# MLP biases as a broadcast tensor operand instead of a per-partition scalar in the PSUM evacuations

## The chip, the cores and the metric

One core of one Trainium2 chip. The metric is device time in microseconds (us), from the first to the last instruction of the program on that core. Times of different kernels are compared only where they were taken in the same rounds on the same chip.

## The reference, cut to what matters

A transformer-like block: layer norm, 32-head attention and an MLP on the same normalised input, joined by a gate.

```python
def _A_ref(x, wqkv, wo):            # attention, S=2048, D=1024, 32 heads of 32
    ...
    p = _softmax(scores, axis=-1)
    o = jnp.einsum("bhqk,bhkd->bhqd", p, v)
    return ... @ wo

def _B_ref(x, w1, b1, w2, b2):      # MLP, F=3584
    y = _layernorm(x, axis=-1)
    h = _gelu(jnp.einsum("bsd,df->bsf", y, w1) + b1)
    return jnp.einsum("bsf,fd->bsd", h, w2) + b2

x = A_x
xn = _layernorm(x, axis=-1)
s = _A_ref(xn, A_wqkv, A_wo)
g = _silu(_B_ref(xn, B_w1, B_b1, B_w2, B_b2))
return x + s * g
```

The biases `b1` and `b2` belong to the feature, and the products are stored with features on the partitions. So within one tile a bias is one number per partition, the same for every column.

## The kernel before

Python builds a list of operations for each engine. A helper `op` records what an operation reads and writes, sets the semaphore waits from that, and advances a small model clock by the cost `c` (in ns). The model clock decides where deferred VectorE work (square, cube, gate) and the tanh of ScalarE are put between the rest.

The main loop runs 512 units. In each, TensorE computes attention scores (`s_unit`, line 869 of the kernel), then one piece of a projection or MLP product (line 395), then the attention-value products of the unit before (lines 898 and 901). ScalarE takes the exponentials (line 881). All pieces in the main part accumulate in one PSUM bank, number 7: before the next product may write there, VectorE must have read the last one out. (PSUM is where TensorE's products are written in this kernel, `ps` in the profile; reading a finished product out of it is called its evacuation here.)

```python
def fin(bk):                                   # first MLP product, one of 168 evacuations
    ...
    take(kx, ku)
    run_dq(pg.ready("vector", r=[("b", bk)]) + TOL)      # deferred VectorE work that fits
    x0 = op("vector", lambda e: e.tensor_scalar(xb[:, 0:n], bank(bk, 0, n), b1T[:, f:f + 1], None, op0=ALU.add),
       r=[("b", bk), "b1"], w=[kx], c=217 + 1.042 * n)   # line 548
    ...
    later(square, x0.t + 34.0, (m2, 0))        # deferred: square, cube; then tanh on ScalarE, then gate
```
```python
def fin(bk):                                   # second MLP product, one of 48 evacuations
    ...
    x0 = op("vector", lambda e: e.tensor_scalar(zh[:, 0:n], bank(bk, 0, n), 0.25, b2h[:, nb:nb + 1], op0=ALU.mult, op1=ALU.add),
       r=[("b", bk), "b2"], w=[kz], c=217 + 1.042 * n)   # line 605
```

The width `n` is 352 columns in two thirds of the pieces and 320 in one third.

The softmax here doesn't subtract the row's maximum and nothing guards it: scores larger than these inputs give would overflow.

## Time and profile before

| | before |
|---|---|
| time, median of 4 runs (1089.04 to 1090.72) | 1089.69 us |
| span of the profiled run | 1086.9 us |
| TensorE busy | 1077.7 us, 99% |
| ScalarE busy | 1043.6 us, 96% |
| VectorE busy | 627.6 us, 58% |
| chain that ended last | PE 57%, ACT 42% |

Three of those four runs were known when the prediction was written; their median was 1089.52. A busy share says how full an engine is; the chain says whose work the end waited for. VectorE is on neither list as a bound. In the profile's lines PE is TensorE, PEld its loads of weights (29156, as many as matmuls; one opens each product), DVE VectorE and ACT ScalarE; L548 is line 548 of the kernel.

### The profile page before, as it was taken

What the parts mean: (1) busy time and instruction counts of PE and PEld (TensorE: products, weight loads), DVE (VectorE), ACT (ScalarE), POOL (GpSimd) and SP (SyncE); (2) the same over time, 40 slices, a digit from 0 to 9 for tenths busy, and PEclk for the clock granted to TensorE, in tenths of its full rate; (3) what the DMA queues carried; (4) which work ended last, traced back from release to release, by engine and by line L of the source; (5) the groups of instructions that cost most, each with busy time, mean ns of one, the idle gap of its engine ahead of it and who ended that gap; (6) DMA issues with size and microseconds to landing.
All of it is one profiled execution on the core that took longest, in us unless ns stands there. A gap on an engine that the chain in (4) does not pass through costs nothing.

```text
span 1086.9 us, 61820 instructions
## 1 busy us (share of the span) xinstructions
PE 1077.7 (99%) x29156; PEld 701.4 (65%) x29156; DVE 627.6 (58%) x1396; ACT 1043.6 (96%) x1197; POOL 22.5 (2%) x69
## 2 busy tenths in 40 slices
PE   9999999999999999999999999999999999999998
PEld 6766666666666666666666666666666666666665
DVE  8488843477732576642377743378733387635556
ACT  7899998999999999999999999999999999999993
POOL 4400000000000000000000000000000000000000
PEclk9999999999999999999999999999999999999999
DMA  8944355413474224345233264423264243685444
GB/s 243 178 134 139 116 165 154 126 52 110 118 155 123 67 60 125 104 104 149 90 100 102 70 165 113 125 81 109 81 132 119 91 119 108 194 202 110 108 92 124
DMA packets 209336, 131.92 MB, mean 121 GB/s; under 512 B 52538, under 2 KB 200250, under 8 KB 209082
## 3 DMA queue, kind: packets, MB, share of 16 engines
q1 hardware_dynamic: 209082, 127.97, 43.5%
q8 instruction: 228, 3.74, 1.5%
q14 instruction: 26, 0.21, 0.1%
HBM read 104.87 MB, written 12.06 MB: 108 GB/s over the span
## 4 chain that ended last, share of the span: by engine, by line
PE 57%; ACT 42%; DVE 0%; DMA 0%; issue 0%; POOL 0%; SPq 0%
ACT P L881 38%; PE ps L395 33%; PE ps L869 9%; PE ps L898 6%; PE ps L901 6%; ACT u L565 3%; PE ps L687 1%; PE ps L703 1%; ACT thz L609 0%; DMA OT<-in_A_x_dram 0%; PE ps L386 0%; DVE wq L669 0%; ACT hT L714 0%; DVE zh L605 0%; DVE wq L671 0%
## 5 line engine op out<-in xcount | busy, mean ns | idle before, releaser
L881 ACT ACTIVATE P<-ps 128x1024 bf16<-128x1024 f32 x1024 | 968.1, 1080 | 8.7 <-PE ps L869 3.9
L898 PE MATMUL ps<-P,VP 128*32 128x256 bf16 x4096 | 256.4, 273 | 0.0
L901 PE MATMUL ps<-P,ones 128*32 128x256 bf16 x4096 | 256.3, 273 | 0.0
L395 PE MATMUL ps<-yTc,war 128*32 128x352 bf16 (+1 forms) x5376 | 225.5, 309 | 0.5 <-issue 0.5
L395 PE MATMUL ps<-hT,war 128*32 128x352 bf16 (+1 forms) x5376 | 225.3, 309 | 0.0
L869 PE MATMUL ps<-QT,KT 32*128 32x256 bf16 x4096 | 203.3, 273 | 2.7 <-ACT P L881 0.2
L395 PEld LDWEIGHTS ps<-yTc,war 128*32 128x32 bf16 x5376 | 127.4, 96 | 74.9 <-DVE xb L548 19.2
L395 PEld LDWEIGHTS ps<-hT,war 128*32 128x32 bf16 x5376 | 127.9, 96 | 73.9 <-issue 25.1
L869 PEld LDWEIGHTS ps<-QT,KT 32*128 32x128 bf16 x4096 | 60.7, 92 | 114.4 <-issue 60.4
L605 DVE TENSOR_SCALAR zh<-ps,b2h 128x352 f32<-128x352 f32 (+1 forms) x48 | 27.4, 572 | 182.6 <-PE ps L395 182.6
L548 DVE TENSOR_SCALAR xb<-ps,b1T 128x352 f32<-128x352 f32 (+1 forms) x168 | 96.2, 573 | 48.9 <-PE ps L395 43.9
L571 DVE SCALAR_TENSOR_TENSOR hT<-u,xb 128x352 bf16<-128x352 f32 (+1 forms) x168 | 84.4, 510 | 67.6 <-ACT u L565 67.6
L898 PEld LDWEIGHTS ps<-P,VP 128*32 128x32 bf16 x4096 | 109.3, 97 | 20.4 <-issue 1.3
L901 PEld LDWEIGHTS ps<-P,ones 128*32 128x32 bf16 x4096 | 109.2, 97 | 18.7
L395 PE MATMUL ps<-xnT,wq 128*32 128x352 bf16 (+1 forms) x2688 | 112.7, 309 | 0.0
L395 PEld LDWEIGHTS ps<-xnT,wq 128*32 128x32 bf16 x2688 | 63.7, 96 | 37.2 <-DVE xb L548 9.1
L558 DVE SCALAR_TENSOR_TENSOR u<-u,xb 128x352 f32<-128x352 f32 (+1 forms) x168 | 82.5, 509 | 1.9
L554 DVE TENSOR_TENSOR u<-xb 128x352 f32<-128x352 f32 (+1 forms) x168 | 82.5, 507 | 0.7
L565 ACT ACTIVATE u<-u 128x704 f32<-128x704 f32 (+1 forms) x84 | 71.4, 855 | 0.0
L395 PE MATMUL ps<-xnT,OT 128*32 128x352 bf16 (+2 forms) x1568 | 62.9, 306 | 0.2 <-DVE wq L669 0.2
L395 PE MATMUL ps<-wq,xnT 128*32 128x256 bf16 x1536 | 50.8, 274 | 0.0
L395 PEld LDWEIGHTS ps<-xnT,OT 128*32 128x32 bf16 x1568 | 37.7, 96 | 19.9 <-DVE wq L669 7.7
(61 smaller groups left out, 478.6 us busy)
## 6 DMA issues: line engine op xcount, KB each, us to landing
war<-in_B_w_dram SPq DMA_DIRECT2D x336, 256.0 KB, 3.3
wq<-in_A_wqkv_dram SPq DMA_DIRECT2D x36, 128.0 KB, 2.5
OT<-in_A_x_dram SPq DMA_DIRECT2D x16, 256.0 KB, 5.6
xnT<-in_A_x_dram SPq DMA_DIRECT2D x16, 256.0 KB, 3.2
out_dram<-wq SPq DMA_DIRECT2D x15, 256.0 KB, 2.0
y_scratch<-OT SPq DMA_DIRECT2D x14, 256.0 KB, 2.5
gT_scratch<-gst SPq DMA_DIRECT2D x32, 88.0 KB, 3.2
xnT<-in_A_wo_dram SPq DMA_DIRECT2D x8, 256.0 KB, 4.3
```

The costliest lines, as they stand in the source:

```text
L395: ins = e.matmul(outs(j), lhsT=lhs(j), rhs=rhs, start=start, stop=stop, tile_position=(0, 32 * j), skip_group_check=True)
L548: x0 = op("vector", lambda e: e.tensor_scalar(xb[:, 0:n], bank(bk, 0, n), b1T[:, f:f + 1], None, op0=ALU.add), r=[("b", bk), "b1"], w=[kx] ...
L554: x = op("vector", lambda e: e.tensor_tensor(ub[:, 0:n], xb[:, 0:n], xb[:, 0:n], op=ALU.mult), r=[kx], w=[ku], c=151 + 1.042 * n)
L558: x = op("vector", lambda e: e.scalar_tensor_tensor(ub[:, 0:n], ub[:, 0:n], 1.0 / 0.044715, xb[:, 0:n], op0=ALU.add, op1=ALU.mult), r=[kx, ...
L565: x = op("scalar", lambda e: e.activation(ut[:, :, 0:n], ut[:, :, 0:n], ACT.Tanh, scale=0.7978845608028654 * 0.044715), r=kus, w=kus, c=48 ...
L571: op("vector", lambda e: e.scalar_tensor_tensor(hT[:, fq, 0:n], ut[:, i, 0:n], 1.0, xq[:, 0:n], op0=ALU.add, op1=ALU.mult), r=[kus[i], kq] ...
L605: x0 = op("vector", lambda e: e.tensor_scalar(zh[:, 0:n], bank(bk, 0, n), 0.25, b2h[:, nb:nb + 1], op0=ALU.mult, op1=ALU.add), r=[("b", bk ...
L687: ins = e.matmul(bank(bk, off, off + 256), lhsT=wq[:, which, dc, 0:128], rhs=xnT[:, dc, t0:t0 + 256], start=dc == 0, stop=dc == DC - 1, sk ...
L869: ins = e.matmul(bank(bks[j], kh * 256, (kh + 1) * 256), lhsT=KT[i2][32 * j:32 * j + 32, k0:k0 + 128], rhs=QT[i2][32 * j:32 * j + 32, qb * ...
L881: op("scalar", lambda e, p=p, sl=sl: e.activation(pb[:, 2 * p:2 * p + 2, :, :].rearrange("p a b q -> p (a b q)"), ps[:, sl * 1024:(sl + 1) ...
L898: e.matmul(bankq(ACC, j, 0, QW), lhsT=VP[vp][:, kb, vo + 32 * j:vo + 32 * j + 32], rhs=pb[:, j, kh, :], start=first, stop=False, tile_posi ...
L901: ins = e.matmul(bankq(ACC, j, QW, 2 * QW), lhsT=ones[:, 0:32], rhs=pb[:, j, kh, :], start=False, stop=last, tile_position=(0, 32 * j), sk ...
```

## The change

The intent is to shorten the evacuations that add a bias. The per-partition scalar becomes an ordinary second tensor operand, whose access pattern repeats the one bias of each partition over all columns. The builder's cost of the two evacuations goes from 217 to 165 ns plus 1.042 ns per column.

```diff
-                x0 = op("vector", lambda e: e.tensor_scalar(xb[:, 0:n], bank(bk, 0, n), b1T[:, f:f + 1], None, op0=ALU.add),
-                   r=[("b", bk), "b1"], w=[kx], c=217 + 1.042 * n)
+                x0 = op("vector", lambda e: e.tensor_tensor(xb[:, 0:n], bank(bk, 0, n), b1T[:, f:f + 1].to_broadcast((128, n)), op=ALU.add),
+                   r=[("b", bk), "b1"], w=[kx], c=165 + 1.042 * n)
...
-                x0 = op("vector", lambda e: e.tensor_scalar(zh[:, 0:n], bank(bk, 0, n), 0.25, b2h[:, nb:nb + 1], op0=ALU.mult, op1=ALU.add),
-                   r=[("b", bk), "b2"], w=[kz], c=217 + 1.042 * n)
+                x0 = op("vector", lambda e: e.scalar_tensor_tensor(zh[:, 0:n], bank(bk, 0, n), 0.25, b2h[:, nb:nb + 1].to_broadcast((128, n)), op0=ALU.mult, op1=ALU.add),
+                   r=[("b", bk), "b2"], w=[kz], c=165 + 1.042 * n)
```

## The prediction

1089.52, the median known then, less 0.4 for the direct gain is 1089.1 us. The lengths of the new forms stand on the trace alone: 524 and 490 ns of line 669, and 526 and 492 as an estimate from lines 558 and 554 (519 and 518 ns). The 1 to 6 us allowed for the order, and so the range, follow from no measurement; what one misplaced tanh costs was not measured either. The "half rate" of rival 3 is a supposition; its 330 ns are an estimate, about what 320 columns take once more at the 1.03 ns of the trace.

> **What bounds the kernel now.** I read the page's busy shares first, then the chain of work that ended last, then the groups of VectorE by form, the waits, and last the timeline around single evacuations, because a busy share cannot tell whether a wait of 0.06 us is hidden.
>
> ```profile
> PE 1077.7 (99%) x29156; PEld 701.4 (65%) x29156; DVE 627.6 (58%) x1396; ACT 1043.6 (96%) x1197; POOL 22.5 (2%) x69
> ...
> PE 57%; ACT 42%; DVE 0%; DMA 0%; issue 0%; POOL 0%; SPq 0%
> ```
>
> TensorE and ScalarE are both nearly full and share the whole chain; VectorE, the only engine that the change touches, is 58% busy and has no share of the chain that rounds above 0%. The per-line figures of the chain agree: the bias evacuation of the first MLP product does not appear among the fifteen lines printed, and that of the second is there with 0%. The granted clock is 0.999, so no throttle hides anything.
>
> Next, what one bias evacuation costs beside its neighbours. The groups by form, with the mean in ns as the second number after the bar:
>
> ```profile
> L548 DVE TENSOR_SCALAR xb<-ps,b1T 128x352 f32<-128x352 f32 x112 | 65.4, 584 | 30.5 <-PE ps L395 26.6
> ...
> L548 DVE TENSOR_SCALAR xb<-ps,b1T 128x320 f32<-128x320 f32 x56 | 30.8, 551 | 18.3 <-PE ps L395 17.3
> ...
> L605 DVE TENSOR_SCALAR zh<-ps,b2h 128x352 f32<-128x352 f32 x32 | 18.7, 584 | 141.6 <-PE ps L395 141.6
> ...
> L669 DVE TENSOR_TENSOR wq<-ps,xnT 128x352 f32<-128x352 f32 x32 | 16.8, 524 | 19.4 <-PE ps L395 19.3
> ...
> L605 DVE TENSOR_SCALAR zh<-ps,b2h 128x320 f32<-128x320 f32 x16 | 8.8, 548 | 41.0 <-PE ps L395 41.0
> ```
>
> The two-tensor form from PSUM (L669, of the output projection) takes 524 ns on 352 columns; the form with a per-partition scalar takes 584. That difference of 60 ns is what the change is after.
>
> The waits show one reason to take it seriously. All projection and MLP products of the main part accumulate in the same PSUM bank, so the next product cannot start before the evacuation has read the bank:
>
> ```profile
> PEld ps L395 <- DVE xb L548: 34.7, 164, 0.3
> ...
> PEld ps L395 <- DVE zh L605: 10.1, 48, 0.2
> ```
>
> These are 44.8 us in 212 waits, 0.21 us each. They name VectorE, but 0.21 us is also what the weight loads idle when nothing is waited for ("issue": 29.6 us in 138 times, 0.21 each). So I looked at single instances. Two stretches of the timeline (start, length, engine, line):
>
> ```profile
> 411.35 0.42 DVE L435 CAST VP<-ps 128x256 bf16<-128x256 f32 x1
> ...
> 411.75 0.40 PE L869 MATMUL ps<-QT,KT 32*128 32x256 bf16 x8
> 412.07 0.94 PEld L395 LDWEIGHTS ps<-xnT,wq 128*32 128x32 bf16 x32 [0.21 <-issue]
> ```
> ```profile
> 702.78 0.58 DVE L548 TENSOR_SCALAR xb<-ps,b1T 128x352 f32<-128x352 f32 x1
> ...
> 703.10 0.40 PE L869 MATMUL ps<-QT,KT 32*128 32x256 bf16 x8
> ...
> 703.42 1.02 PEld L395 LDWEIGHTS ps<-yTc,war 128*32 128x32 bf16 x32 [0.21 <-DVE xb L548]
> ```
>
> In the first the evacuation is the short one and ends at 411.77, 0.30 us before the next product starts; in the second it is a biased one and ends at 703.36, 0.06 us before. Yet from the start of the score matmuls (L869) to the start of the next product it is 0.32 us in both. I collected that distance over the whole timeline for every product that follows score matmuls: the median is 0.33 us in each of the seven groups of evacuation (by line and width), and only 2 of the 216 biased evacuations are followed by a distance above 0.36 us (0.39 both times). The sum of all excess over 0.33 us, all groups together, is 0.23 us. So TensorE goes from score matmuls to the next product in its own 0.33 us, and the biased evacuation ends 0.06 us (352 columns) or 0.09 us (320) before that runs out. **It is hidden, by a narrow margin.**
>
> [...] L669 takes 524 and 490. [...] (584 - 551)/32 = 1.03 ns per column for the form of now. [...] Here one bank serves, and the overlap is with the attention matmuls in between; the trace shows it suffices. [...]
>
> **The change, part by part.**
> First MLP product (168 evacuations): a TENSOR_SCALAR with a pointer to the bias becomes a TENSOR_TENSOR whose second operand repeats the bias with step zero. From L669 I expect 524 and 490 ns, so 112 x 60 + 56 x 61 ns = 10.1 us less VectorE.
> Second MLP product (48 evacuations): TENSOR_SCALAR becomes SCALAR_TENSOR_TENSOR, the 0.25 now an immediate. No such form from PSUM is in the trace. From SBUF it costs what TENSOR_TENSOR costs (L558 519 against L554 518 on 352 columns), so I take 526 and 492: 32 x 58 + 16 x 56 ns = 2.8 us less.
> Sum: 12.9 us less VectorE busy, 627.6 to about 614.7 (57% of the span).
> What lies on the path: nearly none. By the distances above at most 0.23 us of TensorE time is lost to any late evacuation. The other consumer is ScalarE, which waits for the biased result of the second product 8 times, 6.3 us in all; each can end 0.06 us earlier, 0.5 us together, if the time isn't lost again at the next exponential. Expected direct gain: 0 to 0.7 us.
> What moves: the builder keeps a model clock and uses it to choose where deferred VectorE work (square, cube, gate) and the tanh of ScalarE go between other work. The cost of the evacuation in this model falls by 52 ns, so here and there one of these is placed one slot earlier or later. No work is added or removed by that, semaphores guard the same data, and the weights' loads follow the products. Some tens of instructions may change places. [...]
>
> **The rivals.**
> (1) The evacuation is the bound after all, through the single bank. For it: 212 waits that name these lines, and margins of only 0.06 us. Against it: the same distance where the evacuation ends 0.30 us early. Were it true, all 216 x 0.06 = 12.9 us would come back, 1076.6 us, 1.2% faster. Even that is not over 2%.
> (2) The new order of the deferred work costs. For it: the list of products is hand-tuned to the present order, and both bounding engines have little slack. Against it: only model times of 52 ns in slots of some 2 us move. I allow 1 to 6 us, so up to 1095; a lucky order gives 1084.
> (3) Reading a step-zero operand is slower than a plain one. For it: the trace has no fp32 two-tensor instruction with such an operand. Against it: L921 transposes with a broadcast input in 443 ns, L914 without one, from PSUM, in 440. At half rate an evacuation would take some 330 ns more than TENSOR_TENSOR, 270 more than now; less the hidden 0.06 us this is 0.2 us x 216 = 45 us on TensorE's path, about 1135. I give it one chance in a hundred.
>
> **Range and chances.** Start from 1089.52, take 0.4 for the direct gain (middle of 0 to 0.7), add nothing for the order, whose sign I can't tell: 1089.1. The width is that of rival 2, three parts in four: 1084 to 1093. A gain over 2% needs under 1067.7, more than even rival 1 has to give: 0.01. A loss over 2% needs over 1111.3, which only rival 3 reaches: 0.015. The rest, 0.975, is within 2%.
>
> **What would show it.** Right: L548 near 524 and 490 ns, L605 near 526 and 492; VectorE busy near 615 us; the chain still split between PE and ACT with DVE at 0%; the distance from score matmuls to the next product still 0.33 us, while the evacuation now ends 0.12 us before it instead of 0.06. Wrong: if that distance shrinks by 0.06 us behind biased evacuations, rival 1 held; if the waits of ScalarE on L605 or of VectorE on tanh grow by several us, rival 2; if L548 is at or above 584 ns, rival 3. The prediction as a whole is wrong if the time leaves 1084 to 1093.

## The result, and the profile after

The changed kernel took 1090.09 us (median of 4 runs, 1089.48 to 1090.35), before 1089.69 us. The ratio is 1.0002, with a 95% interval of 0.9985 to 1.0019: the same. Ratios here are the mean time of one kernel's fast runs over that of the other's in the same rounds, so they are not quite the ratio of the medians quoted.

The page of the changed kernel, its busy shares and its chain:

```profile
PE 1077.4 (99%) x29156; PEld 701.4 (64%) x29156; DVE 615.2 (57%) x1396; ACT 1044.5 (96%) x1197; POOL 22.4 (2%) x69
...
PE 58%; ACT 40%; DVE 0%; DMA 0%; issue 0%; POOL 0%; SPq 0%
```

VectorE is busy 12.4 us less (627.6 to 615.2). No other engine's busy time moved by more than 1 us, and the chain is still TensorE and ScalarE. The groups of the changed kernel by form (busy us, then the mean of one in ns):

```profile
L548 DVE TENSOR_TENSOR xb<-ps,b1T 128x352 f32<-128x352 f32 x112 | 58.7, 524 | 34.9 <-PE ps L395 31.4
...
L548 DVE TENSOR_TENSOR xb<-ps,b1T 128x320 f32<-128x320 f32 x56 | 27.5, 491 | 18.6 <-PE ps L395 17.0
...
L605 DVE SCALAR_TENSOR_TENSOR zh<-ps,b2h 128x352 f32<-128x352 f32 x32 | 16.8, 524 | 142.8 <-PE ps L395 142.8
...
L605 DVE SCALAR_TENSOR_TENSOR zh<-ps,b2h 128x320 f32<-128x320 f32 x16 | 7.8, 488 | 41.3 <-PE ps L395 41.3
```

Each evacuation is some 60 ns shorter (584 to 524 and 551 to 491 on line 548, 584 to 524 and 548 to 488 on line 605). What became of these 60 ns shows in one unit of the changed kernel's timeline (start us, length us, engine, line), the counterpart of the biased one in the prediction:

```profile
703.32 0.52 DVE L548 TENSOR_TENSOR xb<-ps,b1T 128x352 f32<-128x352 f32 x1
...
703.63 0.40 PE L869 MATMUL ps<-QT,KT 32*128 32x256 bf16 x8
...
703.96 1.01 PEld L395 LDWEIGHTS ps<-yTc,war 128*32 128x32 bf16 x32 [0.21 <-DVE xb L548]
```

The evacuation now ends at 703.84, 0.12 us before the next product's weights; before, 0.06 us. The score matmuls start at 703.63 and the product 0.33 us later, as before. The waits of the changed kernel (total us, times, longest) still put most of these gaps down to the bias evacuation:

```profile
PEld ps L395 <- DVE xb L548: 34.2, 162, 0.2
...
PEld ps L395 <- DVE zh L605: 9.9, 47, 0.2
```

That is 44.1 us in 209 waits, against 44.8 in 212 before. If VectorE had really been what ended those gaps, they would have shrunk by up to 12.9 us.

One thing did change more than the eye expects. By the count made for the experiments, 131 of VectorE's 1398 instructions and 42 of ScalarE's 1197 stand at other places in their order; counted again from the two programs, as those outside the longest common sequence of operations with their tiles, it is 95 of 1396 and 20 of 1197. TensorE's order is the same. So the result could be a sum: faster evacuations, and an order that takes the gain back. This is what the experiments separate first.

### The profile page after: what moved, and what is told of

The parts are those of the page before. It is cut to its first block, busy times and chain, and to the rows that moved or that the text cites. A ratio compares the mean times of both kernels' runs of the same rounds, so it can differ in the third digit from the quotient of the medians.

```text
span 1087.7 us, 61820 instructions
## 1 busy us (share of the span) xinstructions
PE 1077.4 (99%) x29156; PEld 701.4 (64%) x29156; DVE 615.2 (57%) x1396; ACT 1044.5 (96%) x1197; POOL 22.4 (2%) x69
## 4 chain that ended last, share of the span: by engine, by line
PE 58%; ACT 40%; DVE 0%; DMA 0%; issue 0%; POOL 0%; SPq 0%
ACT P L881 36%; PE ps L395 34%; PE ps L869 9%; PE ps L898 6%; PE ps L901 6%; ACT u L565 3%; PE ps L687 1%; PE ps L703 1%; ACT thz L609 0%; DMA OT<-in_A_x_dram 0%; PE ps L386 0%; DVE wq L669 0%; ACT hT L714 0%; DVE wq L671 0%; ACT hT L713 0%
## 5 line engine op out<-in xcount | busy, mean ns | idle before, releaser
L605 DVE SCALAR_TENSOR_TENSOR zh<-ps,b2h 128x352 f32<-128x352 f32 (+1 forms) x48 | 24.6, 512 | 184.1 <-PE ps L395 184.1
L548 DVE TENSOR_TENSOR xb<-ps,b1T 128x352 f32<-128x352 f32 (+1 forms) x168 | 86.2, 513 | 53.5 <-PE ps L395 48.4
```

The lines of the kernel that those rows point to most:

```text
L548: x0 = op("vector", lambda e: e.tensor_tensor(xb[:, 0:n], bank(bk, 0, n), b1T[:, f:f + 1].to_broadcast((128, n)), op=ALU.add), r=[("b", bk ...
L605: x0 = op("vector", lambda e: e.scalar_tensor_tensor(zh[:, 0:n], bank(bk, 0, n), 0.25, b2h[:, nb:nb + 1].to_broadcast((128, n)), op0=ALU.m ...
```

## The experiments

The theory (H): TensorE needs about 0.33 us from the start of the score matmuls to the next product whatever VectorE does, and the biased evacuation ends within that time, so that shortening it gains nothing. The rivals: the evacuation is waited for (1); or the faster form gains and the new order loses it (2). Reading the trace again for the experiments gave a variant of the theory, N: nowhere in the trace of before is there less than 0.05 us between the end of an evacuation and the product behind it, not even in the one instance where the distance was stretched to 0.44 us. If this 0.05 us always passes between an evacuation's end and the product that it releases (below: the signal's own time), the 0.06 us of the prediction is nearly no room at all.

A word on the distances below: for each product that follows score matmuls, the start of the product less the start of the score matmuls, collected from the whole timeline (resolution 0.01 us). "Excess" is what they have above 0.33 us, summed over the 216 biased evacuations. The trace holds a direct sign for H that the prediction did not use: in the unchanged kernel no evacuation of bank 7 starts within the 1.5 us before 120 of these products, and their distance is the same, 0.325 to 0.326 us.

All eight runs gave correct results, except the last, which is wrong.

### Form alone

The new instructions, with the old costs in the builder's model. Every engine then has the order of the kernel before, checked instruction by instruction.

```diff
-                   r=[("b", bk), "b1"], w=[kx], c=165 + 1.042 * n)
+                   r=[("b", bk), "b1"], w=[kx], c=217 + 1.042 * n)
...
-                   r=[("b", bk), "b2"], w=[kz], c=165 + 1.042 * n)
+                   r=[("b", bk), "b2"], w=[kz], c=217 + 1.042 * n)
```

> The new instruction forms with the old costs in the builder's model, so that every engine keeps the order of the kernel before; VectorE alone is faster, by 12.9 us of busy time. Theory H (the evacuation is hidden behind the attention matmuls): 0 to 0.7 us less than before. Rival 1 (the evacuation is waited for): about 12.9 us less. Rival 2 (the faster form helps and the new order takes it back): some us less than before, clearly more than 1.

Measured: 1089.01 us against 1089.33, ratio 0.9999 (0.9987 to 1.0012). VectorE was busy 615.7 us. So the faster form by itself gains nothing that these rounds can see. Rival 1 needed 0.988. Rival 2 needed a gain of clearly more than 1 us here for the order to take away; none is seen, and the interval leaves room for 1.4 us at most.

### Order alone

The old instructions with the new costs: the order of the changed kernel, the evacuations as slow as before.

```diff
-                   r=[("b", bk), "b1"], w=[kx], c=217 + 1.042 * n)
+                   r=[("b", bk), "b1"], w=[kx], c=165 + 1.042 * n)
...
-                   r=[("b", bk), "b2"], w=[kz], c=217 + 1.042 * n)
+                   r=[("b", bk), "b2"], w=[kz], c=165 + 1.042 * n)
```

> The old instruction forms with the new costs in the builder's model: the order of the changed kernel (131 of 1398 VectorE and 42 of 1197 ScalarE instructions moved), the evacuations as slow as before. Theory H: the order is worth under 2 us either way, so the same as both. Rival 2: some us slower than before, and slower than the changed kernel by what the forms gain.

Measured: 1091.01 us against 1089.33, ratio 1.0014 (1.0000 to 1.0028). The order costs at most about 3 us and perhaps 1.7, at the edge of what can be told. It does not balance a hidden gain: the run before shows none.

### The changed kernel again

> The changed kernel again, unaltered, with five rounds, for the fourth corner beside form alone (0.9999) and order alone (1.0014). If the order costs 1.7 us and the form gives back 0.3: 1.4 us slower than before (1.0013). If the order's cost was paid by the slow evacuations only: equal to before within 0.5 us.

Measured: 1090.47 us (1090.43 to 1092.65) against 1090.27, ratio 1.0009 (0.9996 to 1.0021). The corner lies between the two expectations, and all four corners (neither change, form alone, order alone, both) lie within 0.15% of each other. VectorE has 2% of the chain in this run, where the prediction looked for 0%; 1% of it is line 324, the statistics of the layer norm, and not an evacuation. Whether the new order costs 1 us or nothing stays open; it does not matter for the reading.

### How much room the evacuation has: 32, 64 and 96 columns more

The kernel before, in its own order, with the biased evacuations wider than needed. The extra columns are read from the bank and written to wider tiles and never used, so the results stay right. Only the length of the evacuation changes. The run with 32 columns was made after the other two were known.

```diff
-        xb_t = [sb(f"xb{i}", [128, CW], F32) for i in range(NXB)]
+        PAD = 64; xb_t = [sb(f"xb{i}", [128, CW + PAD], F32) for i in range(NXB)]     # 32, 64, 96
...
-                x0 = op("vector", lambda e: e.tensor_scalar(xb[:, 0:n], bank(bk, 0, n), b1T[:, f:f + 1], None, op0=ALU.add),
+                x0 = op("vector", lambda e: e.tensor_scalar(xb[:, 0:n + PAD], bank(bk, 0, n + PAD), b1T[:, f:f + 1], None, op0=ALU.add),
```

(and the same for `zh` on line 605).

> The kernel before with 32 columns more: 617 and 584 ns. Theory N (0.01 us to spare with 352 columns, 0.04 with 320): only the 144 wide ones pass the limit, by 0.023 us: 3.3 us on TensorE; of the two wider runs 60 and 75% of such a sum reached the end, so about 2 us slower. Theory H as predicted (0.06 us to spare): no change. Rival 1 (every ns waited for): 216 x 0.033 = 7 us slower.

> The kernel before, its order kept, with the biased evacuations 64 columns wider than needed (the rest is not used): some 67 ns longer each, 651 and 618 ns. Theory H as the prediction had it, with 0.06 us (352 columns, 144 of them) and 0.09 us (320 columns, 72) to spare: about 1 us slower. Theory N (nearly nothing to spare: the shortest gap from the end of an evacuation to the product behind it is 0.05 us anywhere in the trace, so that this is the signal's own time and 352 columns have 0.01 us to spare, 320 have 0.04): 144 x 0.057 + 72 x 0.027 = 10 us where TensorE alone sets the pace, less where ScalarE does, so 4 to 10 us slower.

> As the run with 64 columns more, with 96: some 100 ns longer each. Theory H with 0.06 and 0.09 us to spare: 144 x 0.04 + 72 x 0.01 = 6 us slower at most. Theory N with 0.01 and 0.04: 144 x 0.09 + 72 x 0.06 = 17 us at most, so 8 to 17 us slower. Rival 1 taken strictly (every ns of an evacuation is waited for): 216 x 0.1 = 22 us slower.

| columns more | length, 352-column pieces | median distance, 352 / 320 | excess, sum | time less before | ratio (95%) |
|---|---|---|---|---|---|
| 0 (before) | 584 ns | 0.33 / 0.33 us | 0.12 us | | |
| 32 | 617 ns | 0.36 / 0.33 us | 3.7 us | 1092.28 - 1090.27 = 2.0 us | 1.0016 (1.0002 to 1.0029) |
| 64 | 651 ns | 0.39 / 0.36 us | 10.7 us | 1095.76 - 1089.33 = 6.4 us | 1.0060 (1.0047 to 1.0073) |
| 96 (4 runs; the others 5) | 684 ns | 0.42 / 0.39 us (line 548) | 17.7 us | 1102.60 - 1089.33 = 13.3 us | 1.0119 (1.0105 to 1.0133) |

One unit of the run with 64 columns more, from its timeline:

```profile
705.74 0.65 DVE L548 TENSOR_SCALAR xb<-ps,b1T 128x416 f32<-128x416 f32 x1 [0.34 <-PE ps L395]
...
706.06 0.40 PE L869 MATMUL ps<-QT,KT 32*128 32x256 bf16 x8
706.44 1.01 PEld L395 LDWEIGHTS ps<-yTc,war 128*32 128x32 bf16 x32 [0.27 <-DVE xb L548]
```

The evacuation ends at 706.39 and the weights follow 0.05 us later. Now VectorE is what ends the gap: it has grown from 0.21 to 0.27 us. The same holds wherever the distance is stretched: in the run with 96 columns more that is behind 212 of the 216 biased evacuations, and the weights follow 0.051 to 0.053 us after the end of every one of them. This is how a real wait looks, against the apparent ones of before.

Here the room is measured. Theory N's sums were 3.3, 10 and 17 us; the excess is 3.7, 10.7 and 17.7 (3.5, 10.2 and 17.6 when counted to the ns). So a biased evacuation of 352 columns had about 0.01 us to spare and one of 320 about 0.04; the prediction's 0.06 and 0.09 contain a signal time of 0.05 us. With 0.06 and 0.09, 64 columns more would have cost about 1 us, and they cost 6.4.

Of the excess 54, 60 and 75% reach the end; the first figure is loose, as the interval of that run goes from 0.2 to 3.2 us. The rest is likely taken up where ScalarE sets the pace: the score matmuls' waits for the exponentials fall as the evacuations grow. From the lists of waits of the kernel before, and of the runs with 64 and with 96 columns more, in that order:

```profile
PEld ps L869 <- issue: 60.4, 286, 0.2
PEld ps L869 <- ACT P L881: 53.4, 222, 0.5
```
```profile
PEld ps L869 <- issue: 68.6, 325, 0.2
...
PEld ps L869 <- ACT P L881: 40.9, 183, 0.4
```
```profile
PEld ps L869 <- issue: 74.9, 355, 0.2
...
PEld ps L869 <- ACT P L881: 32.7, 151, 0.4
```

Most of that fall is only a change of name: gaps of 0.21 us that were put down to the exponentials are now put down to nothing ("issue"). The two lines together fall from 113.8 to 109.5 and 107.6 us, by 4.3 and 6.2 us; the excess that did not reach the end is 4.3 and 4.4 us. This fits in size, but no run isolates it.

### The new form, 64 columns wider

```diff
+        PAD = 64; ...
...
-                x0 = op("vector", lambda e: e.tensor_tensor(xb[:, 0:n], bank(bk, 0, n), b1T[:, f:f + 1].to_broadcast((128, n)), op=ALU.add),
+                x0 = op("vector", lambda e: e.tensor_tensor(xb[:, 0:n + PAD], bank(bk, 0, n + PAD), b1T[:, f:f + 1].to_broadcast((128, n + PAD)), op=ALU.add),
```

(and the same for `zh` on line 605, with `scalar_tensor_tensor`).

> The new forms in the old order, 64 columns wider than needed: 524 + 67 = 591 and 557 ns, 7 ns more than the kernel before has with the old forms. If only the length of an evacuation counts, TensorE behind it loses at most 144 x 0.007 = 1 us, so 0 to 1 us slower than before, although the old forms with the same 64 columns were 6.4 us slower. If the two-tensor form costs anything else [...], it is slower than that.

Measured: 1090.44 us against 1090.27, ratio 0.9999 (0.9986 to 1.0011). The group of line 548 in this run:

```profile
L548 DVE TENSOR_TENSOR xb<-ps,b1T 128x416 f32<-128x416 f32 x112 | 66.2, 591 | 30.5 <-PE ps L395 27.4
```

Sixty-four columns more with the new form cost nothing that can be seen (1.2 us at most, by the interval); with the old form they cost 6.4 us. So the length is what counts, and not the columns themselves or the form. At 591 ns the median distance behind line 548 is 0.328 us instead of 0.326: this is the knee, where the room just runs out. This is also what the change did buy: some 60 ns of room, in which this kernel has nothing to put.

### The new form, 64 columns narrower (wrong on purpose)

```diff
-        PAD = 64; xb_t = [sb(f"xb{i}", [128, CW + PAD], F32) for i in range(NXB)]
+        PAD = -64; xb_t = [sb(f"xb{i}", [128, CW], F32) for i in range(NXB)]
```

(with all of these tiles set to zero by GpSimd once, in the prologue).

> Wrong result on purpose: the new forms in the old order, evacuating 64 columns fewer than needed (the tiles are set to zero once at the start by GpSimd, so that all reads are defined): 457 and 424 ns, 67 ns below the changed kernel. Theory N: the evacuation ended before TensorE needs the bank anyway, so no gain, within 1 us of before. Rival 1, or any cost of VectorE's busy time as such (another 14 us off it): up to 14 us faster than the form alone.

Measured: 1089.35 us against 1090.27, ratio 0.9997 (0.9984 to 1.0009). The result is wrong (relative error 0.13). The median distance is still 0.33 us in every group, though the evacuations take 457 and 425 ns on line 548 and VectorE is down to 606.7 us busy. So the flat side goes on: from 584 ns down to 457 there is nothing to gain, while from about 590 upwards (352-column pieces) nearly every further ns stretches the distance (0.36, 0.39 and 0.42 us at 617, 651 and 684 ns).

No version beats both kernels. Form alone is at 0.9999, and the narrow run at 0.9997 (0.9984 at best) shows that a still shorter evacuation gains nothing that can be seen.

## Why the prediction was right

**VectorE's saving.** Right within 1 ns for the first product (524 and 491 against 524 and 490 predicted) and within 4 ns for the second (524 and 488 against 526 and 492). The busy time came out at 615.2 us, 614.7 predicted. The step-zero operand took no longer than a full second tensor (524 and 491 ns on line 548, 524 and 490 on line 669): rival 3 is dead.

**That nearly none of it lies on the path.** Right, and shown from three sides: form alone 0.9999, the widths above with a stretched distance, the narrow run below with none. Rival 1 falls with that.

**The gain through ScalarE.** Its waits for line 605 fell from 6.3 to 5.8 us, the half us named, and were 5.8 us in the run with the form alone. But they were 7.6 us when the changed kernel was run again, so the match is in part luck and this gain is not shown. In the time it can't be seen.

**The order.** Its sign was left open and the allowance was 1 to 6 us; it is at most about 3. "Some tens" of moved instructions was low for VectorE, where 95 or 131 moved, by the way of counting.

**What failed in it.** One step was wrong, although the forecast did not hang on it: "the biased evacuation ends 0.06 us (352 columns) or 0.09 us (320) before that runs out". The distance from the end of an evacuation to the start of the product behind it was not all room: 0.05 us of it passes even where the product does wait (0.051 to 0.053 us in the run with 96 columns more), so the real room was about 0.01 and 0.04 us. The evidence was in the trace: nowhere was that distance below 0.05 us, not even in the three places where the product came late (0.38, 0.39 and 0.44 us after the score matmuls). The prediction's "the trace shows it suffices", of the single bank, holds with no more than this room. The same slip is in rival 3's sum, which takes 0.06 us off as hidden. The kernel was thus at the edge, not near it: the change gained nothing, but a change of about the same size in the other direction (67 ns) costs 6.4 us. The range of 1084 to 1093 us came from the unknown sign of the order, not from this margin, so that the step could be wrong and the time still fall inside.

## What to carry to other kernels

212 waits of 0.21 us named the biased evacuations, and some 60 ns off each evacuation gained nothing (ratio 1.0002): an event named in a list of waits need not be what holds the engine. So compare the same gap behind a short and a long evacuation, and if it is equal, the producer isn't the bound. To know how much room a hidden step has, lengthen it in small steps without changing anything else: the flat part and the knee show the room, and the slope shows what lies behind. And where a builder's cost model orders the work, a changed cost is a second change in the same diff; run the form and the order apart before crediting either.
